# Loading v by heads, moving one step's second products, and shifting the w2 splits and a visit in a fused attention and mixture kernel

## The chip, the cores and the metric

The kernel runs on one core of a Trainium2 chip. The metric is the device time of one execution in microseconds (us). The kernel before was run three times: 449.62, 449.82 and 450.59 us, median 449.82 us.

## The reference

Four batches of four heads, 1088 positions and head dimension 32 go through a polynomial sketch attention; its output, 4352 tokens of 128 features, goes into a mixture of four two-layer experts with 1024 hidden units each.

```
phi(x)  = outer(S1 x, S2 x), flattened to 64 features      # S1, S2 are 8 x 32
kv      = sum over s of phi(k)_s v_s^T ;  z = sum over s of phi(k)_s
attn    = (phi(q) kv) / (phi(q) z + 1e-6)                  # per batch and head
x       = attn, heads side by side                         # 4352 x 128
p       = domain_probs / (sum of domain_probs + 1e-9)
out     = sum over e of p[:, e] * relu(x w1[e]) w2[e]      # 4 experts
```

Everything is fp32.

## The kernel before, in words

**The mixture.** The tokens are cut into chunks of 128, 448, 512, seven times 448, and 128. Each chunk takes sixteen steps: expert e is the step's number divided by four, and each step handles two blocks of 128 hidden units, one in each of two half-steps. Step i has half-steps 2i and 2i + 1, so half-step 33 is the second one of step 16, the first step of the second chunk. `first` makes the hidden units of a step. In the middle chunks w1 and x are split in three parts of shorter mantissa, and each block is three matmuls on TensorE (PE): L1175 and L1176 (names xa, wa and xb, wb), then, after ScalarE (ACT) has scaled the sum at L1177, L1227 (xd, wd). ScalarE then applies relu (L1231 or L1236), and VectorE (DVE) makes the lower parts of the hidden units (L1203 and L1206). In the first and the last chunk, called plain, the matmuls are plain fp32 and cut into halves of 64 rows or columns (`both` and `on_side`, L262).

**The second products.** `second` multiplies hidden units by w2 and adds up in a PSUM accumulator. The list `due` gives the half-step at which the second products of a step are issued. For plain chunks this is 2i + 5, but 2i + 7 for step 14 (`i == NQ - 2`), so that step 14's second products stand right before those of step 15 at half-step 35, eight instructions of 64 x 128 in all. With `w2` split in parts (`vab`, `vb`, `vd`), the later chunks use L1296 for the second products; in chunk 1 experts 0 and 1 use whole fp32 w2 (L1277). The parts of w2 are made by one split on ScalarE (L928, `vab<-w_sb`) and joins on DVE (L931: `vab`, `vb`, then `vd`), at the half-steps of `W2_AT`, one pair for each of the experts 2, 3, 0 and 1.

**The attention.** What is needed to start, the keys and values of batch 0 and its first queries, is made in `start`. Keys are turned (`kn` to `kT`), projected (fs) and multiplied (kp); `value_copy` spreads the values `vn` into `vx` on ScalarE (L423, L428), and PE sums kp times vx (L262, `h<-vx,kp`). The query factors are copied from PSUM (L1040, qb) and multiplied on DVE. Later work of the attention is cut into pieces with costs in a plan, which `work` hands out in half-steps. The units of queries after the first ones are the list `later`; the first of them (index w = 0; batch 0, 512 tokens) is called the third unit here. Its way is: its queries are turned and projected (`unit_project`, which writes `qs` to DRAM as `qd<-qs`, L790, and reads it back spread out, as `qp<-qd`, L797, and `qb<-qd`, L802), its two products are made on DVE (`unit_product`, L811), and its visit does the products `kvx` times `qp` on PE (L262) together with the projection `qT` times `sx` of the unit after it. `LAND` is 6: the third unit's products and visit are not handed out before LAND + 1 half-steps have passed since `unit_project`.

**The loads.** SyncE (SP) issues nearly all DMAs in program order: s_raw, k, q and v of batch 0, then the weights w1 (L159) and w2 (L172), then the k, q and v of later batches (`load_batch`: batch 1 after step 5, batch 2 after step 24), gates, and the `qd` traffic. `load_v` fills the tile `vn`, 128 partitions of 1088 floats. Partition 32a + g holds, for each head, positions 34g + 8a to 34g + 8a + 7; two small transfers (L137) bring the remaining two positions of each g. DMAs take eight semaphore lanes in turn, so the issue of one waits until the one that used its lane before, eight DMAs earlier, has landed.

Of the kernel before, what the change touches and what calls it, by code (L numbers as in the profile page):

```python
# [17 lines left out]
def _ap(t, p0: int, np_: int, off: int, free):  # L18

    p = list(t.ap)[0]  # L20
    return bass.AP(t.tensor, t.offset + p0 * p[0] + off, [[p[0], np_]] + [list(d) for d in free])
# [3 lines left out]
def kernel(  # L25
# [24 lines left out]
    nc = tc.nc  # L50
# [3 lines left out]
    B, H, S, D = q.shape  # L54
    E, DM, F = w1.shape
    R = 8
    R2 = 2 * R
    G = S // 32
# [3 lines left out]
    NQ = E * FB // 2  # L62
# [4 lines left out]
    LAND, EARLY = 6, 14  # L67
# [21 lines left out]
        ("b", 1, 1, 16), ("d", 1, 1, 17), ("b", 2, 0, 16), ("d", 2, 0, 17), ("b", 2, 1, 17), ("d", 2, 1, 18),  # L89
        ("a", 3, 1, 17), ("b", 3, 0, 19), ("b", 3, 1, 19), ("d", 3, 0, 20), ("d", 3, 1, 20),  # L90
    ]
    W2_AT = (36, 38), (41, 43), (45, 47), (65, 67)
    TOKENS_AT = 11, 12

    CHUNKS = [P, 448, 512] + [448] * 7 + [P]
# [32 lines left out]
    def load_v(b):  # L128
        t = lpool.tile([P, H * NT * D], F32, tag="vn", name="vn")
        base = v.offset + b * H * S * D  # L130
        for a in range(4):
            nc.sync.dma_start(
                _ap(t, 32 * a, 32, 0, [[8 * D, H], [1, 8 * D]]),
                bass.AP(v.tensor, base + 8 * a * D, [[G * D, 32], [S * D, H], [1, 8 * D]]),
            )
        for a in range(2):
            nc.sync.dma_start(  # L137
                _ap(t, 32 * a, 32, 1024, [[D, H], [1, D]]),
                bass.AP(v.tensor, base + (32 + a) * D, [[G * D, 32], [S * D, H], [1, D]]),
            )  # L140
        return t
# [35 lines left out]
    def in_three(b):  # L177
        return b in THREE
# [10 lines left out]
    def split_at(b):  # L189
        return (THREE if in_three(b) else OTHER).index(b)  # L190

    def second_weight(e, b):

        at = split_at(b)
        return w2_of[e, 0 if in_three(b) else 1][:, DM * at : DM * (at + 1)]
# [359 lines left out]
    def key_sums(b):  # L555
        sums[b] = held(psum(ps_h, "h"))
        for p in range(2):
            key_sum(b, p, sums[b])
# [207 lines left out]
    def unit_turn(w):  # L766

        b, c, n, u = later[w]
        turned[w] = query_turn(b, c, n)
        if w and u == len(UNITS[b]) - 1 and b + 1 < B:  # L770
            load_rows(q, b + 1, "qn")
# [36 lines left out]
    def unit_product(w, p):  # L808

        n, (qp, qb) = later[w][2], factors[w]  # L810
        nc.vector.tensor_tensor(out=qp[p][:, 0:n], in0=qp[p][:, 0:n], in1=qb[p][:, 0:n], op=ALU.mult)  # L811
# [12 lines left out]
    def vector_us(n):  # L824

        return 0.16 + n * 1.04e-3
# [3 lines left out]
    def add(cost, run, name, after=None):  # L830

        plan.append((cost, run, name, after))

    def lay_plan():

        of_first = queries(0, P, UNITS[0][1])
        costs = [0.62] * 9 + [0.05] * 4 + [0.4, 0.55, 0.6, 0.1, 0.1]
        distances = {12: ("first8", 3), 13: ("first12", 1), 16: ("first15", 2), 17: ("first16", 2)}
        for at, cost in enumerate(costs):
            add(cost, lambda: next(of_first, None), f"first{at}", distances.get(at))  # L840
        covers.append((len(plan), P + UNITS[0][1]))
        add(vector_us(later[0][2]), lambda: unit_turn(0), "qturn", ("start", 2 * NQ - 2))
        add(0, lambda: None, "wait", ("start", 2 * NQ + 2))
        keys = {}
        for b in range(1, B):
            now_on, plan[:] = list(plan), []
            key_pieces(b)
            keys[b], plan[:] = list(plan), now_on
        for w, (b, c, n, u) in enumerate(later):
            if b == 0:  # L850
                plan.extend(keys[1][:9])
            else:
                at = {(1, 0): (1, 9, 13), (1, 1): (2, 0, 3), (1, 2): (2, 3, 5), (2, 1): (3, 0, 3), (2, 2): (3, 3, 9)}
                if (b, u) in at:
                    k, z0, z1 = at[b, u]
                    plan.extend(keys[k][z0:z1])
                if b == 1 and u == 0:
                    blocked = key_end(b)
            more = w + 1 < len(later)
            if more:  # L860
                add(vector_us(later[w + 1][2]), lambda w=w: unit_turn(w + 1), "qturn")
            for p in range(2):
                add(vector_us(n), lambda w=w, p=p: unit_product(w, p), "product", ("visit", LAND if w else LAND + 1))

            last = 0 < b < B - 1 and u == len(UNITS[b]) - 1
            if last:
                plan.extend(keys[b + 1][(5, 9)[b - 1] :])

            def visit(w=w, more=more, then=b + 1 if last else None):
                if then:  # L870
                    key_sums(then)
                if w == 1:
                    key_sums(1)
                    blocked()
                if more:
                    unit_project(w + 1)
                unit_visit(w)

            add(0.1, visit, "visit", ("products" if last else "product", 3))
            if last:  # L880
                key_end(b + 1)
            add(0.4, lambda w=w: inverse.__setitem__(w, attend_inverse(*products[w])), "inverse", ("visit", 1))
            add(vector_us(n), lambda w=w: over.__setitem__(w, attend_scale(*products[w], inverse.pop(w))), "scale")
            add(vector_us(n), lambda w=w: unit_out(w), "out")
            covers.append((len(plan), S * b + c + n))
# [214 lines left out]
    hid, acc, total = {}, {}, {}  # L1100
    NP = FB // 2

    def plain(m):
        return m in (0, NC - 1)
# [133 lines left out]
    def second(i, j=None):  # L1238

        m, kq = steps[i]  # L1240
        n, (e, f) = CHUNKS[m], divmod(kq, NP)
        hd = hid[i]
        if plain(m):

            if f == 0:
                acc[m] = psum(ps_o, f"o{e % 2}")
            for j in range(2):
                for _ in range(2):
                    on_side(
                        lambda s: acc[m][half[s], 0:DM],  # L1250
                        lambda s: hd[j][:, HP * s : HP * s + HP],
                        lambda s: second_weight(e, 2 * f + j),
                        start=(f == j == 0),
                        stop=(f == NP - 1 and j == 1),
                    )
            if f == NP - 1:
                p_e = ends[:, 1 if m else 0, e : e + 1]
                if e == 0:
                    total[m] = mpool.tile([P, P], F32, tag="end", bufs=1, name="end")
                    nc.vector.tensor_scalar(  # L1260
                        out=total[m][:, :], in0=acc[m][:, 0:DM], scalar1=p_e, scalar2=None, op0=ALU.mult
                    )
                else:
                    nc.vector.scalar_tensor_tensor(
                        out=total[m][:, :], in0=acc[m][:, 0:DM], scalar=p_e, in1=total[m][:, :], op0=ALU.mult, op1=ALU.add
                    )
                if e == E - 1:
                    t, to = (B * S - P, [[DM, P], [1, DM]]) if m else (0, [[G * DM, 32], [1, 4 * DM]])
                    nc.sync.dma_start(bass.AP(out.tensor, out.offset + t * DM, to), total.pop(m)[:, :])
            return  # L1270
        if whole(m, e):
            if f == 0 and j == 0:
                acc[m, e] = None, psum(ps_o, f"o{e % 2}")
            for j in range(2) if j is None else (j,):
                k = 2 * f + j
                o1 = acc[m, e][1][:, 0:n]
                nc.tensor.matmul(o1, second_weight(e, k), hd[j], start=(k == 0), stop=(k == FB - 1))  # L1277
            return
# [119 lines left out]
    for what, e, h, step in SPLITS:  # L1398
        at_step(step, lambda p=(what, e, h): weight_part(*p))
    for e, at in zip((2, 3, 0, 1), W2_AT):  # L1400
        parts_of = second_weight_parts(e)
# [25 lines left out]
    due, closed = [], [None]  # L1427
# [19 lines left out]
    def to_due(i):  # L1447

        m, kq = steps[i]
        e, f = divmod(kq, NP)  # L1450
        if plain(m):
            due.append((2 * i + (7 if i == NQ - 2 else 5), 2 * i, 0, i, None, None))
        elif whole(m, e):
            late = (0, 0, 0, 0, 1, 1, 1, 1)[2 * f : 2 * f + 2] if e else (0, 0)
            due.extend((2 * i + 3 + j + late[j], 2 * i, j, i, j, None) for j in range(2))
        elif f == 0:
            for at, (p, slot) in enumerate(deal_of(m, e).items()):
                k = int(p[1])
                due.append((2 * i + slot, 2 * i, at, i + k // 2, k % 2, p[0]))
        due.sort(key=lambda d: d[:3])  # L1460

    for i in range(len(steps) + LA):
        if i < len(steps):
            m, kq = steps[i]
# [89 lines left out]
```

## Time and profile before

| | |
|---|---|
| median of three runs | 449.82 us (449.62 to 450.59) |
| the profiled execution | 449.77 us, span 448.0 us, so 1.77 us outside the span |
| granted TensorE clock | 1.0 in every slice |
| busy in the span | PE 99%, weight loads 83%, DVE 83%, ACT 75%, POOL 29% |
| first matmul of the mixture on PE | at 13.57 us |
| the v loads of batch 0 | issued 2.10 to 5.17 us, landed 6.15, 6.45, 6.78 and 7.91 us |
| the third unit's qd written | 37.5 and 38.08 us |
| its qb landed | 47.22 us (first set), about 50.5 us (second set) |

A row of the profile names the line of the kernel, the engine, the operation and `out<-in` with the names of the tiles. Times are from the start of the span. A bracket behind a row of the timeline is the time for which the engine stood idle before it and what released it. [...]

### The profile page before, as it was taken

How to read it: one execution, taken by the hardware profiler on the slowest of the kernel's cores; microseconds unless marked ns; L12 is line 12 of the kernel's file. 1: busy time of each engine (PE TensorE's matmuls, PEld its weight loads, DVE VectorE, ACT ScalarE, POOL GpSimd, SP SyncE). 2: the span in 40 equal slices, each digit the busy share in tenths (PEclk: the TensorE clock that was granted, in tenths of full speed). 3: DMA queues.
4: the chain of work that ended last, by engine and by line, in shares of the span. 5: the costliest groups of instructions: out<-in, count | busy, mean ns of one | idle time of the engine just before them, and what ended most of it. 6: DMA issues, size and time to landing. Idle time of an engine off the chain costs nothing.

```text
span 448.0 us, 8698 instructions
## 1 busy us (share of the span) xinstructions
PE 442.2 (99%) x3018; PEld 371.1 (83%) x3018; DVE 371.7 (83%) x634; ACT 334.0 (75%) x710; POOL 130.2 (29%) x211
## 2 busy tenths in 40 slices
PE   9999999999999999999999999999999999999997
PEld 6887678777778888888888888888888888888887
DVE  5998779986988896989879969898889898898853
ACT  4477778966867886778687868788788888888841
POOL 7346123310333132212321322123323313331440
PEclk9999999999999999999999999999999999999999
DMA  6965145014313502252252132421230021016501
GB/s 184 277 181 160 65 122 161 30 46 114 94 53 89 125 23 75 49 136 65 64 125 34 20 110 79 107 66 21 67 80 20 22 66 42 21 35 205 171 1 29
DMA packets 53619, 38.45 MB, mean 86 GB/s; under 512 B 26920, under 2 KB 49640, under 8 KB 53576
## 3 DMA queue, kind: packets, MB, share of 16 engines
q1 hardware_dynamic: 52776, 37.31, 31.4%
q0 software_dynamic: 576, 0.53, 0.5%
q8 instruction: 23, 0.38, 0.4%
q14 instruction: 20, 0.16, 0.1%
q10 hardware_dynamic: 224, 0.07, 0.1%
HBM read 32.68 MB, written 5.21 MB: 85 GB/s over the span
## 4 chain that ended last, share of the span: by engine, by line
PE 88%; DMA 4%; DVE 3%; SPq 2%; ACT 1%; issue 0%; POOL 0%; ACTq 0%; DVEq 0%; POOLq 0%
PE o L1296 40%; PE h L1227 13%; PE h L1175 13%; PE h L1176 13%; PE h L262 6%; PE o L262 2%; DMA qb<-qd 1%; DMA w_sb<-in_moe_w_dram 1%; SPq L172 1%; PE o L1277 1%; PE h L457 1%; DMA dp<-in_moe_domain_probs_dram 1%; DVE wb L931 1%; DVE wd L931 0%; DMA qd<-qs 0%
## 5 line engine op out<-in xcount | busy, mean ns | idle before, releaser
L1177 ACT ACTIVATE h<-h 128x448 f32<-128x448 f32 (+1 forms) x288 | 155.4, 540 | 72.0 <-PE h L1176 68.0
L1203 DVE SCALAR_TENSOR_TENSOR hb<-h,ha 128x448 fp32r<-128x448 f32 (+1 forms) x213 | 130.2, 622 | 39.2 <-ACT ha L1231 36.6
L1206 DVE SCALAR_TENSOR_TENSOR hd<-ha,hb 128x896 fp32r<-128x896 f32 (+2 forms) x111 | 123.5, 1113 | 11.3 <-PE o L1296 2.2
L1175 PE MATMUL h<-xa,wa 128*128 128x448 f32 (+1 forms) x288 | 131.4, 456 | 0.0
L1231 ACT ACTIVATE ha<-h 128x448 fp32r<-128x448 f32 (+1 forms) x213 | 116.6, 547 | 0.0
L1335 POOL TENSOR_TENSOR ev<-ev,gate 128x256 f32<-128x256 f32 (+1 forms) x54 | 47.6, 881 | 214.3 <-DVE ev L1328 205.4
L1227 PE MATMUL h<-xd,wd 128*128 128x448 f32 (+1 forms) x288 | 107.5, 373 | 1.1 <-ACT h L1177 1.0
L1176 PE MATMUL h<-xb,wb 128*128 128x448 f32 (+1 forms) x288 | 105.9, 368 | 0.0
L1296 PE MATMUL o<-ha,vab 128*128 128x448 f32 (+1 forms) x204 | 76.2, 374 | 0.0
L1175 PEld LDWEIGHTS h<-xa,wa 128*128 128x128 f32 x288 | 54.2, 188 | 18.2 <-issue 13.1
L1176 PEld LDWEIGHTS h<-xb,wb 128*128 128x128 f32 x288 | 54.2, 188 | 17.8 <-issue 13.7
L1227 PEld LDWEIGHTS h<-xd,wd 128*128 128x128 f32 x288 | 54.0, 188 | 10.9 <-ACT h L1177 4.2
L1296 PE MATMUL o<-hd,vd 128*128 128x448 f32 (+1 forms) x204 | 60.1, 369 | 0.0
L1296 PE MATMUL o<-hid,w_sb 128*128 128x448 f32 (+1 forms) x118 | 54.7, 545 | 0.0
L1296 PE MATMUL o<-hb,vb 128*128 128x448 f32 (+1 forms) x136 | 50.1, 368 | 0.0
L1337 POOL TENSOR_TENSOR total<-total,ev 128x256 f32<-128x256 f32 (+1 forms) x54 | 46.1, 854 | 4.2
L1236 ACT ACTIVATE hid<-h 128x448 f32<-128x448 f32 (+1 forms) x75 | 41.4, 552 | 1.0 <-PE h L1227 0.8
L1296 PEld LDWEIGHTS o<-ha,vab 128*128 128x128 f32 x204 | 38.3, 188 | 4.1
L1296 PEld LDWEIGHTS o<-hd,vd 128*128 128x128 f32 x204 | 38.1, 188 | 3.7
L1335 POOL TENSOR_TENSOR total<-ev,gate 128x256 f32<-128x256 f32 (+1 forms) x18 | 12.8, 730 | 70.7 <-issue 50.6
L1296 PEld LDWEIGHTS o<-hb,vb 128*128 128x128 f32 x136 | 25.5, 188 | 2.1
L1296 PE MATMUL o<-hb,vab 128*128 128x448 f32 (+1 forms) x68 | 25.3, 372 | 0.0
(153 smaller groups left out, 458.4 us busy)
## 6 DMA issues: line engine op xcount, KB each, us to landing
gate<-gates SPq DMA_DIRECT2D x22, 224.0 KB
kn<-in_k_dram SPq DMA_DIRECT2D x4, 544.0 KB
vn<-in_v_dram SPq DMA_DIRECT2D x16, 128.0 KB
w_last<-in_moe_w_dram SPq DMA_DIRECT2D x4, 512.0 KB
w_sb<-in_moe_w_dram SPq DMA_DIRECT2D x3, 512.0 KB
w_sb<-in_moe_w_dram SPq DMA_DIRECT2D x6, 256.0 KB
qp<-qd SPq DMA_DIRECT2D x6, 224.0 KB
qb<-qd SPq DMA_DIRECT2D x6, 224.0 KB
```

The lines of the kernel that those rows point to most:

```text
L262: nc.tensor.matmul(out(s), weights(s), moving(s), **flags)
L1175: nc.tensor.matmul(g, wa[:, e, w], xa, start=True, stop=False)
L1176: nc.tensor.matmul(g, wb[:, e, w], xb, start=False, stop=True)
L1177: nc.scalar.activation(g, g, ACTF.Copy, scale=1.0 + R12)
L1203: nc.vector.scalar_tensor_tensor(out=hb, in0=g, scalar=0.0, in1=high, op0=ALU.max, op1=ALU.subtract)
L1206: nc.vector.scalar_tensor_tensor(out=d2, in0=a2.bitcast(F32), scalar=R12, in1=b2.bitcast(F32), op0=ALU.mult, op1=ALU.subtract)
L1227: nc.tensor.matmul(g, w, x, start=False, stop=True, skip_group_check=True)
L1231: nc.scalar.activation(ha, g, ACTF.Relu, scale=NEAR)
L1236: nc.scalar.activation(hid[i][j], g, ACTF.Relu)
L1296: nc.tensor.matmul(acc[m, e][o][:, 0:n], w, h, start=first_one, stop=last)
L1335: nc.gpsimd.tensor_tensor(out=to[:, x], in0=ev[:, x], in1=g[:, x], op=ALU.mult)
L1337: nc.gpsimd.tensor_tensor(out=total[m][:, x], in0=total[m][:, x], in1=ev[:, x], op=ALU.add)
```

## The change

Three things change. `load_v` brings the values of a batch by heads: each of the four large transfers has one head, all 128 partitions, 256 floats for each. The source is read in four groups (a) of 32 rows (g). The runs stay 1 KB and the tile's contents stay the same. The second products of step 14 are due at 2i + 5 like the others of a plain chunk, and they are two matmuls on full 128 x 128 tiles in place of four on halves. `W2_AT` gives the splits of experts 3 and 0 one half-step less, and the third unit's products and visit wait LAND + 2 half-steps in place of LAND + 1.

```diff
-    W2_AT = (36, 38), (41, 43), (45, 47), (65, 67)
+    W2_AT = (36, 38), (40, 42), (44, 46), (65, 67)
...
     def load_v(b):
         t = lpool.tile([P, H * NT * D], F32, tag="vn", name="vn")
         base = v.offset + b * H * S * D
-        for a in range(4):
+        for h in range(H):
             nc.sync.dma_start(
-                _ap(t, 32 * a, 32, 0, [[8 * D, H], [1, 8 * D]]),
-                bass.AP(v.tensor, base + 8 * a * D, [[G * D, 32], [S * D, H], [1, 8 * D]]),
+                t[:, 8 * D * h : 8 * D * (h + 1)],
+                bass.AP(v.tensor, base + S * D * h, [[8 * D, 4], [G * D, 32], [1, 8 * D]]),
             )
...
             for p in range(2):
-                add(vector_us(n), lambda w=w, p=p: unit_product(w, p), "product", ("visit", LAND if w else LAND + 1))
+                add(vector_us(n), lambda w=w, p=p: unit_product(w, p), "product", ("visit", LAND if w else LAND + 2))
...
             for j in range(2):
+                if i == NQ - 2:
+                    o, w = acc[m][:, 0:DM], second_weight(e, 2 * f + j)
+                    nc.tensor.matmul(o, hd[j], w, start=False, stop=False)
+                    continue
                 for _ in range(2):
                     on_side(
...
         if plain(m):
-            due.append((2 * i + (7 if i == NQ - 2 else 5), 2 * i, 0, i, None, None))
+            due.append((2 * i + 5, 2 * i, 0, i, None, None))
```

On each engine the order moves as follows. On PE, two 128 x 128 instructions stand between L1176 and L1227 of half-step 33, the group of eight halves two half-steps later has four, and the third unit's visit stands one half-step later. On DVE, the joins `vab` and `vb` of an expert now stand ahead of the third unit's first product, where they stood behind it, and its second product stands ahead of the next expert's joins. On ACT, each L928 split of the two moved experts stands one half-step earlier.

## The prediction

> **What bounds the kernel now.** I read the busy times first, then what TensorE waited for, then the timelines around those waits, then DMA landings. The page's busy list and the waits of PE:
>
> ```profile
> PE 442.2 (99%) x3018; PEld 371.1 (83%) x3018; DVE 371.7 (83%) x634; ACT 334.0 (75%) x710; POOL 130.2 (29%) x211
> ```
>
> ```profile
> PE h L1227 <- ACT h L1177: 1.0, 2, 0.8
> ...
> PE h L262 <- DMA w_sb<-in_moe_w_dram: 0.5, 1, 0.5
> ```
>
> TensorE fills the span, the granted clock is full in every slice, and after about 58 us PE waits on nothing. So a microsecond comes or goes only by PE instructions saved or by a stall in the first 58 us. There the start is a chain of other engines and loads: first MoE matmul of PE at 13.57 us, and behind it the weights. The two L1227 waits are these (timeline of PE; start, duration, engine, line, operation, in brackets the idle time and its releaser):
>
> ```profile
> 29.80 0.36 PE L1176 MATMUL h<-xb,wb 128*128 128x448 f32 x1
> 30.37 0.47 PE L1227 MATMUL h<-xd,wd 128*128 128x448 f32 x1 [0.21 <-ACT h L1177]
> ...
> 49.27 0.37 PE L1176 MATMUL h<-xb,wb 128*128 128x448 f32 x1
> 50.39 0.47 PE L1227 MATMUL h<-xd,wd 128*128 128x448 f32 x1 [0.76 <-ACT h L1177]
> ```
>
> Undisturbed, L1227 starts 0.20 us after L1176 (30.88 to 31.08). So the first place loses 0.57 - 0.20 = 0.37 us, the second 1.12 - 0.20 = 0.92 us. The second has its cause in VectorE and ScalarE:
>
> ```profile
> 47.34 0.69 DVE L811 TENSOR_TENSOR qp<-qp,qb 128x512 f32<-128x512 f32 x1 [2.76 <-DMA qb<-qd]
> 47.95 0.42 DVE L931 SCALAR_TENSOR_TENSOR vab<-w_sb,vab 128x256 fp32r<-128x256 f32 x1
> 48.28 0.68 DVE L931 SCALAR_TENSOR_TENSOR vb<-w_sb,vab 128x512 fp32r<-128x512 f32 x1
> ```
>
> ```profile
> 49.06 0.85 ACT L928 ACTIVATE vab<-w_sb 128x768 fp32r<-128x768 f32 x1 [1.13 <-DVE vb L931]
> ```
>
> VectorE stood 2.76 us before a product whose factor had not landed, the w2 joins were queued behind it, ScalarE's split waited for them, and L1177, which PE needs, was queued behind the split.
>
> **Second products of step 14.** Eight half-width instructions of step 15's and 14's group become four there, and two full 128x128 ones stand before the L1227 that waited. Price: the sixteen half-width records of that group (one row of the PE timeline, 31.78, 1.09 us, 0.27 for one) run 0.055 us apart, two per instruction, so four instructions are 0.44 us; the full-width fp32 form has L457 as nearest row, 8 records of 0.89 us on the chain, four instructions, so two are 0.44 us. No saving in rate: the two lie in the 0.57 us gap, make the L1227 wait no more (0.20 + 0.44 = 0.64, 0.07 later than now), and 0.44 leaves the later group. Net -0.37 us (-0.27 to -0.5; a restart after a wait showed up to 0.1 us).
>
> **W2 splits and the visit.** The splits go one half-step earlier, the third unit's visit one later. On DVE the joins now stand ahead of the waiting product, so the split of 49.06 no longer waits: -0.92 us, and with it a smaller one at 57.36 (L1177 behind the split of 56.38, 0.15 us), together -1.07, with a restart -1.17. What hides the moved product: the second qp product starts at 50.63 when its factor lands, ends near 51.3; PE would come to the second kvx matmuls, a half-step later, near 51.3 to 51.8 once the stall is gone. That cover is thin: each microsecond by which the factors land later is a microsecond of PE wait. The later pieces move by a half-step; by the order on PE and ACT the small late stalls (0.17 at 80.31, 0.14 at 140.83) only move: 0, within 0.2 either way. The second joins are queued behind the second product, same term.
>
> **The v loads.** Four transfers of 128 KB remain, of 1 KB runs. Before: 32 partitions each, outermost loop of 32 on both sides. After: 128 partitions, but the source's outermost loop counts 4. The trace has such a form: the qb loads (L802, outermost source loop of 4). Windows of 1 us while they run (last two columns: share of the 16 DMA engines, GB/s), and the chain's piece:
>
> ```profile
> 46.00:47.00 1.00, 1.00 (x6) 0.77 (x5) 0.00 (x0) 0.94 (x4) 0.00 (x0) 1.00 0.26 100
> 47.00:48.00 1.00, 1.00 (x5) 0.61 (x4) 0.66 (x2) 0.93 (x2) 0.00 (x0) 1.00 0.26 98
> 48.00:49.00 1.00, 1.00 (x6) 0.66 (x4) 1.00 (x4) 0.00 (x0) 0.00 (x0) 1.00 0.26 98
> ```
>
> ```profile
> 40.88 6.34 DMA qb<-qd
> ```
>
> A share of 0.26 is four engines of 16, and each qb transfer ends with four engine completions on its semaphore, while an old v transfer ends with 16 and a gate load (outermost loop of 8) with 8. I take the count of the outermost loop as the number of engines: v would run on four. [...]
>
> Price: 512 packets over four engines, 128 each. A qb packet of 2 KB takes about 84 ns at 98 GB/s over four; by bytes 42 ns for 1 KB. The page's hardware queue gives 31.4% of 448.0 us x 16 for 52776 packets, 43 ns for a mean of 707 B; the line through that and 84 ns puts 1 KB at 52 ns. Old v packets, 16 engines at once, took 62 to 77. I take 47, between the nearest two: 6.0 us; the ends are 5.4 and 9.9. The engines are through with k and q at about 4.7 us (first completions of both: 4.3 to 4.9), so v lands at 10.7 (10.1 to 14.6) instead of 7.91. Need: the vx copies start at
>
> ```profile
> 8.35 0.63 ACT L423 COPY vx<-vn 128x512 f32<-128x512 f32 x1
> ```
>
> with 0.43 us of slack before PE's key sums feel it. Then fs, qb (L1040), kp, qp and all PE work shift by 10.7 - 8.35 - 0.43 = 1.9 us (1.3 to 5.8). Behind v on those four engines stand the last pieces of v and q and the first weights: their data began near 9.4, after near 11.6, +2.2 us. SP's queue counts as well: the first v transfer no longer waits for a landed k (now 1.7 us), but w1's and w2's issues (L159, L172) now wait for lanes that v holds; ScalarE's dp issues wait for s_raw, q and v lanes, hidden as they end before fs. PE waited 0.75 us (start to start) for w1 at 19.78, landing 20.45; with both delays near 2 that wait stays, so the larger one sets the shift: +2.2 us (0.9 to 5.8).
>
> Batch 1's v (issued 22.6 to 26.1 now) goes over four engines too, landing near 39 instead of 32.2. The gates, and the qd<-qs write of the third unit (issue 35.43, with the shift about 37.5, on a lane a v transfer holds), stand behind: 1.4 to 2 us later, so also qp, qb and the product. With the thin cover above PE then waits 0.5 to 1.0 at its kvx matmuls: +0.7 (0 to 3). Batches 2 and 3 load with several microseconds to spare: 0.
>
> Sum: +2.2 - 0.37 - 1.17 + 0.7 = +1.36. The profiled execution was 449.77 (span 448.0, 1.77 outside), 0.05 below the median 449.82: 451.13 for it, 451.2 for the median. My case's own range: 450.0 to 452.6.
>
> **The rivals.** *v still spreads over 16 engines* (faster): then it lands in time, the weights go out earlier, the w1 wait at 19.78 goes, capped at 0.35 since the kvx matmuls behind it wait for DVE's product at 20.50. -0.37 - 1.17 - 0.35 = -1.9: 447.9. For: 128 destination partitions, and only the source loop is short. Against: qb also had 32 partitions on its destination and got four. It decides if v lands before 8.8. [...]
>
> *Four engines, but quick, and no late qd* (same): at 42 ns v lands at 10.1, shift 1.3 to 1.5, -1.54 from the rest: 449.5 to 449.9. It needs the gates and qd to slip past v.
>
> *Four engines at the old packet time* (slower by more): landing at 12.6 to 14.6, shift 3.8 to 5.8, qd later by another 2: 453 to 456. For: the early v shares the memory with k and q. Against: with four engines fewer packets are in flight at once.
>
> *The joins' move does nothing* (part of the change fails): product and split only exchange places and PE waits 0.9 at kvx; my case plus 1.0, 452.2.
>
> **Chances.** My case 0.46 (with the fourth), 16 engines 0.20, quick 0.18, old packet time 0.16. What a measurement can tell from no change is 0.2%, 0.9 us. Of my case 0.04 falls under +0.9 and of the quick 0.05 above; faster 0.20, same 0.17, slower 0.63. The range takes the fast case's 447.9 and leaves out the upper part of the last: 447.9 to 454.0. Cases of both signs hold much; the likeliest one's own range is above.
>
> **What would show it.** DMA share near 0.25 from 5 to 10.7 us; L423 starting at 10 or later with a wait on vn; PE idle before L262 h<-vx,kp; PE's first x_first matmul near 15.5; no L1227 wait at the two places; L790 issued late, with kvx waiting for qp. If the share at 5 to 8 us stays above 0.6 and L423 stays at 8.4, v is not on four engines and my sum is wrong by 2.9 us. If L1227 waits again near 52, the joins' step is wrong.

## The result, and the profile after

The changed kernel takes 452.45 us (median of six runs, 451.46 to 453.35), the kernel before beside it 449.72 us (six runs, 448.62 to 450.59). The ratio is 1.0063, interval 1.0041 to 1.0084: 2.8 us slower, between 1.8 and 3.8. The profiled execution took 452.79 us, span 451.0.

The page's busy times and the waits of PE:

```profile
PE 443.1 (98%) x3014; PEld 372.3 (83%) x3014; DVE 371.4 (82%) x634; ACT 334.1 (74%) x710; POOL 125.9 (28%) x211
```

```profile
PE h L262 <- ACT vx L423: 3.4, 1, 3.4
...
PE h L262 <- DVE kvx L513: 0.3, 1, 0.3
PE h L262 <- DVE qp L610: 0.2, 1, 0.2
```

The two waits of L1227 and the one for w1 are gone; one wait of 3.44 us for the copies of v has come. The chain of work that ended last now runs through the last of the four v transfers, at its start:

```profile
3.97 7.99 DMA vn<-in_v_dram
12.74 3.87 PE h L262 x72
```

ScalarE's and PE's timelines say what hangs on it (in brackets the idle time before and its releaser):

```profile
12.06 0.63 ACT L423 COPY vx<-vn 128x512 f32<-128x512 f32 x1 [2.49 <-DMA vn<-in_v_dram]
```

```profile
12.74 0.49 PE L262 MATMUL h<-vx,kp 128*64 128x66 f32 x4 [3.44 <-ACT vx L423]
```

The copy was at 8.35 us and did not wait. Each v transfer's lane shows one semaphore event soon after its issue (3.20 us for the first, issued at 2.09) and four later ones, here called its completions; the last of the four, its landing, comes at 7.13, 8.54, 10.59 and 11.96 us. The windows (columns: the stretch and its length, then busy time of PE, PEld, DVE, ACT, POOL with counts, granted TensorE clock, share of the DMA engines, GB/s) show a share of 0.22 and 0.28, about four engines of 16, in two stretches in which little but v is in flight, an idle PE, and something that the prediction did not have, a clock cut to half:

```profile
5.00:6.00 1.00, 0.98 (x13) 0.38 (x13) 0.94 (x3) 0.70 (x2) 0.90 (x4) 1.00 0.22 53
...
10.00:11.00 1.00, 0.00 (x0) 0.00 (x0) 0.41 (x2) 0.00 (x0) 0.64 (x2) 1.00 0.28 91
11.00:12.00 1.00, 0.00 (x0) 0.00 (x0) 0.00 (x0) 0.00 (x0) 0.00 (x0) 1.00 0.91 147
12.00:13.00 1.00, 0.26 (x4) 0.26 (x6) 0.18 (x2) 0.94 (x3) 0.13 (x1) 0.77 0.61 238
13.00:14.00 1.00, 1.00 (x22) 1.00 (x22) 1.00 (x5) 0.67 (x3) 1.00 (x3) 0.50 0.79 292
14.00:15.00 1.00, 1.00 (x24) 1.00 (x23) 0.93 (x5) 0.00 (x0) 0.78 (x5) 0.50 0.76 221
15.00:16.00 1.00, 1.00 (x24) 1.00 (x24) 0.41 (x1) 0.00 (x0) 0.81 (x4) 0.52 1.15 291
```

A clock of 0.77, 0.50, 0.50 and 0.52 in these four windows makes 0.46, 1, 1 and 0.96 us at half clock, about 3.4 us.

The places of the old L1227 waits, in PE's timeline:

```profile
33.93 0.37 PE L1176 MATMUL h<-xb,wb 128*128 128x448 f32 x1
34.13 0.60 PE L1250 MATMUL o<-w_sb,hid 128*128 128x128 f32 x4
34.51 0.47 PE L1227 MATMUL h<-xd,wd 128*128 128x448 f32 x1
...
52.99 0.36 PE L1176 MATMUL h<-xb,wb 128*128 128x448 f32 x1
53.19 0.36 PE L1227 MATMUL h<-xd,wd 128*128 128x448 f32 x1
```

From L1176 to L1227 it is 0.58 us at the first place, with the two full-tile matmuls inside (0.57 before, without them), and 0.20 at the second (1.12 before). Where the same matmul stands in both profiled executions, the changed kernel's PE is late by 3.33 us at the first vx,kp (12.74 and 9.41), 4.88 at the first x_first (18.45 and 13.57), 4.15 at L1175 of half-step 32 (33.22 and 29.07), 3.71 four half-steps later, 2.43 once the visit is past (60.85 and 58.43 at L1175), 3.0 at the end.

### The profile page after: what moved, and what is told of

Same layout as the page of the kernel before. It is cut to its first block, busy times and chain, and to the rows that moved or that the text cites. A ratio compares the mean times of both kernels' runs of the same rounds, so it can differ in the third digit from the quotient of the medians.

```text
span 451.0 us, 8694 instructions
## 1 busy us (share of the span) xinstructions
PE 443.1 (98%) x3014; PEld 372.3 (83%) x3014; DVE 371.4 (82%) x634; ACT 334.1 (74%) x710; POOL 125.9 (28%) x211
## 4 chain that ended last, share of the span: by engine, by line
PE 94%; DVE 2%; DMA 2%; SPq 1%; issue 0%; ACT 0%; ACTq 0%; DVEq 0%
PE o L1300 40%; PE h L1227 13%; PE h L1175 13%; PE h L1176 13%; PE h L262 7%; PE o L1281 3%; PE o L262 2%; DMA vn<-in_v_dram 2%; PE h L457 1%; DVE qp L610 0%; SPq L132 0%; DVE qa L903 0%; PE h L1145 0%; DVE hd L1206 0%; DVE rd L642 0%
## 5 line engine op out<-in xcount | busy, mean ns | idle before, releaser
L1177 ACT ACTIVATE h<-h 128x448 f32<-128x448 f32 (+1 forms) x288 | 155.3, 540 | 71.7 <-PE h L1176 67.3
L1206 DVE SCALAR_TENSOR_TENSOR hd<-ha,hb 128x896 fp32r<-128x896 f32 (+2 forms) x111 | 123.4, 1112 | 10.4 <-PE o L1300 1.6
L1175 PE MATMUL h<-xa,wa 128*128 128x448 f32 (+1 forms) x288 | 131.4, 456 | 0.0
L1227 PE MATMUL h<-xd,wd 128*128 128x448 f32 (+1 forms) x288 | 107.2, 372 | 0.1
L1339 POOL TENSOR_TENSOR ev<-ev,gate 128x256 f32<-128x256 f32 (+1 forms) x54 | 46.1, 854 | 216.5 <-DVE ev L1332 206.7
L1176 PE MATMUL h<-xb,wb 128*128 128x448 f32 (+1 forms) x288 | 105.9, 368 | 0.0
L1175 PEld LDWEIGHTS h<-xa,wa 128*128 128x128 f32 x288 | 54.2, 188 | 18.3 <-issue 12.9
L1176 PEld LDWEIGHTS h<-xb,wb 128*128 128x128 f32 x288 | 54.2, 188 | 17.7 <-issue 13.7
L1227 PEld LDWEIGHTS h<-xd,wd 128*128 128x128 f32 x288 | 54.0, 188 | 8.5 <-ACT h L1177 2.0
L1341 POOL TENSOR_TENSOR total<-total,ev 128x256 f32<-128x256 f32 (+1 forms) x54 | 43.9, 813 | 4.2
```

What stands on the lines that cost most here:

```text
L1175: nc.tensor.matmul(g, wa[:, e, w], xa, start=True, stop=False)
L1176: nc.tensor.matmul(g, wb[:, e, w], xb, start=False, stop=True)
L1177: nc.scalar.activation(g, g, ACTF.Copy, scale=1.0 + R12)
L1206: nc.vector.scalar_tensor_tensor(out=d2, in0=a2.bitcast(F32), scalar=R12, in1=b2.bitcast(F32), op0=ALU.mult, op1=ALU.subtract)
L1227: nc.tensor.matmul(g, w, x, start=False, stop=True, skip_group_check=True)
L1339: nc.gpsimd.tensor_tensor(out=to[:, x], in0=ev[:, x], in1=g[:, x], op=ALU.mult)
```

## The experiments

The theory: the source's outermost loop of four puts each v transfer on four DMA engines, and that alone makes the kernel slower; the rest gains. The rivals: loading by heads or onto 128 partitions is slow in itself, and a second one, that the two other parts gain only in a kernel whose start is late. Ratios are against the kernel before, run beside the others; in 25, 22 and 11 such runs its median was 449.16, 449.32 and 449.41 us. A difference in us is the ratio's distance from 1 times that median. The ratios are not the quotients of the two medians and lie up to 0.0007 from them.

**The changed kernel with the old v loads (e1_old_v).**

```diff
-        for h in range(H):
+        for a in range(4):
             nc.sync.dma_start(
-                t[:, 8 * D * h : 8 * D * (h + 1)],
-                bass.AP(v.tensor, base + S * D * h, [[8 * D, 4], [G * D, 32], [1, 8 * D]]),
+                _ap(t, 32 * a, 32, 0, [[8 * D, H], [1, 8 * D]]),
+                bass.AP(v.tensor, base + 8 * a * D, [[G * D, 32], [S * D, H], [1, 8 * D]]),
```

> The changed kernel with the old v loads. Theory (the v loads on four engines cost all that is lost, the other two parts gain what the trace of after shows, 0.43 and 1.28 us): the start is that of before, first mixture matmul near 13.6 us, no L1227 wait at half-steps 33 and 44, and the time is 449.7 - 1.7 = 448.0 us (447.7 to 448.4). Rival (the two parts gain only because the late start gave DVE and DMA time to run ahead): the stall near 50 us comes back in another place and the time is 449 to 449.7 us.

448.06 us, ratio 0.9969 (0.9957 to 0.9981): 1.4 us faster than before (0.9 to 1.9; 1.1 by the medians). That is the theory's time and not the 449 to 449.7 us of the rival: the two other parts gain with an early start too. Sixteen completions for each v transfer where the change had four, L423 at 8.3 us, no L1227 wait. This version beats both kernels.

**Only the v loads (e2_v_only).** The diff of e1 the other way, on the kernel before.

> The kernel before with only the new v loads. Theory: v lands near 12 us, PE idles over 3 us and then runs at half clock, the first mixture matmul comes near 18.4, the wait for w1 near 19.8 is gone (-0.7): 449.7 + 4.1 = 453.9 us, up to 454.4 with the late drift seen in after. Rival (as in the prediction: a delay that the weights and later waits swallow): 451.5 to 452.5 us.

452.87 us, ratio 1.0076 (1.0061 to 1.0090): 3.4 us slower (2.7 to 4.0; 3.7 by the medians). That lies between the two expectations: the v loads cost here somewhat less than the theory's 4.1. In its profiled run v landed at 10.9, PE waited 2.04 us and the clock stayed at 1.0; two of its six runs had a mean clock of 0.996, and they are the slowest (453.49 and 453.70). The wait of L1227 for the split stayed, and grew:

```profile
52.79 0.47 PE L1227 MATMUL h<-xd,wd 128*128 128x448 f32 x1 [1.27 <-ACT h L1177]
```

**Only the second products (e3_second_only).**

```diff
+                if i == NQ - 2:
+                    o, w = acc[m][:, 0:DM], second_weight(e, 2 * f + j)
+                    nc.tensor.matmul(o, hd[j], w, start=False, stop=False)
+                    continue
...
-            due.append((2 * i + (7 if i == NQ - 2 else 5), 2 * i, 0, i, None, None))
+            due.append((2 * i + 5, 2 * i, 0, i, None, None))
```

> The kernel before with only the second products of step 14 in full tiles at half-step 33. Theory (they fill the wait before L1227): 0.4 us less, 449.3 us (449.1 to 449.5). Rival (the wait for L1177 only moves or the gain is taken by the stall near 50 us, whose end is set by a DMA): no change, 449.7.

449.28 us, ratio 1.0001 (0.9990 to 1.0012): no gain. The time itself is the theory's, but the kernel before took 449.16 us beside it, so the ratio speaks for the rival. The trace says why. Against before, PE is 0.44 us early at half-step 32 (run to run, below), 0.87 early at half-step 36, so the part does its 0.43; and 0.41 early after this row:

```profile
49.98 0.47 PE L1227 MATMUL h<-xd,wd 128*128 128x448 f32 x1 [1.22 <-ACT h L1177]
```

The wait that was 0.76 us is 1.22. Behind it stand the split, the joins, the product and at the end a qb load. It landed at 46.80 us where it was 47.22, so 0.42 us earlier, while PE came 0.87 earlier. The rival was right: alone, the gain is given back 15 us later.

**Only the w2 splits and the visit (e4_shift_only), and each of the two (e7_w2_only, e8_visit_only).**

```diff
-    W2_AT = (36, 38), (41, 43), (45, 47), (65, 67)
+    W2_AT = (36, 38), (40, 42), (44, 46), (65, 67)       # e4, e7
...
-    ... ("visit", LAND if w else LAND + 1))
+    ... ("visit", LAND if w else LAND + 2))              # e4, e8
```

> The kernel before with only the w2 splits and the third unit's visit shifted. Theory (joins ahead of the waiting product): the wait of 0.92 us at 49.3 and the one of 0.15 at 57.4 go, 1.1 to 1.3 us less, 448.5 us. Rival (thin cover: the second product's factor lands at 50.5 and PE comes to kvx too early): a wait for qp of 0.3 to 0.8 us at the kvx matmuls, 449.0 to 449.4 us.

> The kernel before with only the w2 splits shifted, the visit as before. Theory (it is the order of the joins before the product that removes the stall): the first product now waits behind or ahead of joins by its own due time; joins first: the stall of 0.92 goes, but PE comes to the visit earlier and waits for qp's second half, landing 50.5: net gain 0.3 to 0.9 us. Rival (the visit's shift does it all): no change, 449.7.

> The kernel before with only the third unit's products and visit one half-step later. Theory: the products come behind the joins of experts 3 but ahead of those of expert 0 in half; the stall of 0.92 us goes or halves, 0.4 to 1.1 us less. Rival (the splits' shift does it all): no change, 449.7.

Both: 448.42 us, ratio 0.9979 (0.9970 to 0.9987), 0.9 us faster (0.6 to 1.3), somewhat less than the theory's 1.1 to 1.3. The visit alone: 448.84, ratio 0.9990 (0.9981 to 0.9999), 0.45 faster, at the low end of its theory. The splits alone: 449.94, ratio 1.0011 (1.0002 to 1.0020), 0.5 slower, which neither the theory nor the rival had. All three traces have lost the 0.92 us wait at the split. In the one with the splits alone PE is 1.63 us ahead of before at that L1227, 0.7 of it from the start; then two long waits in PE's timeline take that away, and it is 0.2 behind:

```profile
50.88 0.69 PE L262 MATMUL h<-kvx,qp 128*64 128x66 f32 x16 [0.37 <-DVE qp L811]
...
70.31 0.47 PE L1227 MATMUL h<-xd,wd 128*128 128x448 f32 x1 [1.14 <-ACT h L1177]
```

```profile
69.20 0.63 ACT L928 ACTIVATE xa<-ring 128x512 fp32r<-128x512 f32 x1 [1.23 <-DMA ring<-xd]
```

The first is the thin cover of the prediction: the visit, not shifted, comes before the second product. At the second, an L1177 is queued behind ScalarE's split of the next chunk's x, which waits for its load (ring<-xd). That load landed at 69.18 us, 68.66 in the kernel before, while PE was 1.14 ahead; why it did not come earlier with PE was not followed. In the two kernels with the visit shifted neither shows. So the shift of the visit is the part that pays. That the splits add to it beside it is likely and not shown: the intervals of e4 and e8 overlap.

**A loop of 32 written as 4 times 8 (e6_loop48).**

Against the kernel of e1:

```diff
-                bass.AP(v.tensor, base + 8 * a * D, [[G * D, 32], [S * D, H], [1, 8 * D]]),
+                bass.AP(v.tensor, base + 8 * a * D, [[8 * G * D, 4], [G * D, 8], [S * D, H], [1, 8 * D]]),
```

> The changed kernel with the old v loads (32 partitions each, all heads, same bytes and packets), but the source's outer loop of 32 written as 4 times 8. Theory (the count of the outermost loop is the number of engines): each transfer ends with four engine completions, v lands near 11 to 14 us, time within 1 us of the changed kernel (452.5). Rival (it is the order by heads or the 128-partition destination that makes the new loads slow): v lands near 8 us with 16 completions and the time is that of the changed kernel with old v loads, near 448.

448.03 us, ratio 0.9970 (0.9958 to 0.9982), the four v transfers landed by 8 us, with 16 completions for each transfer. By the numbers that is the rival's outcome, but the run does not tell the two apart: with 16 completions and not the change's four, the run says nothing of transfers on four engines. The outer step is eight inner steps, so the two loops are one even loop of 32, and the 16 completions are those of that loop in e1. It is e1 again.

**Heads and 128 partitions, with other outermost loops (e9_heads8, e10_heads16).** Same transfers, packets and destinations as in the change; only the source positions differ. Both read other positions of v than the attention needs, so they serve for their times alone.

```diff
-                bass.AP(v.tensor, base + S * D * h, [[8 * D, 4], [G * D, 32], [1, 8 * D]]),
+                bass.AP(v.tensor, base + S * D * h, [[4 * G * D, 8], [8 * D + 16, 16], [1, 8 * D]]),   # e9
+                bass.AP(v.tensor, base + S * D * h, [[8 * D + 16, P], [1, 8 * D]]),                    # e10
```

> The changed kernel, v by heads on 128 partitions as there (same four transfers, same 1 KB packets, same destinations), but the source read in an outermost loop of 8 instead of 4, which takes other positions, so keys meet wrong values. Theory (the outermost count sets the engines): eight completions for each transfer, some 0.75 us each instead of 1.5, the last landing near 8.4 to 9.2, vx copies start 8.4 to 9.3, no clock drop, time 448.0 to 449.0. Rival (order by heads or 128 partitions makes the loads slow): v lands near 12 as in the changed kernel, 452.5.

> As the one with an outermost loop of 8, but with one loop of 128 over overlapping positions (wrong values again), same transfers, packets and destinations. Theory: 16 completions for each transfer, the last v landing at 7 to 8 us, the start of the kernel before, time 448.0 (447.6 to 448.5). Rival: v lands near 12, time 452.5.

e10: 447.94 us, ratio 0.9969 (0.9958 to 0.9980). The four transfers landed at 5.59, 5.99, 6.33 and 6.70 us, with 16 completions each, and ScalarE's copy was back in its place, without a wait:

```profile
8.07 0.63 ACT L423 COPY vx<-vn 128x512 f32<-128x512 f32 x1
```

Loading by heads onto all partitions is no slower than the old loads; against the changed kernel on the same chip (451.87, below) only the source's loops and the addresses that they walk through differ, and the difference is 3.9 us. The addresses are nearly consecutive in e10 and 4352 bytes apart in the change. But in the old loads too each partition's runs start 4352 bytes behind the last one's, and those ran with 16 completions and landed by 7.91 us, so runs that lie apart are not slow in themselves. What is left is the loop of four, with its four completions. e9 was meant to run on eight engines. It showed 16 completions and 447.70 us, ratio 0.9963 (0.9949 to 0.9976): 16 times 272 floats are 4352, just its outer step, so it too is one even loop, of 128. So no v load ended with eight completions, and what eight engines would cost was not measured.

**Matmuls in the gap (e5_fill, e12_fill), and the changed kernel again (e11_after).**

```diff
-        for i in range(3):
+        for i in (0, 1, 2) * 3:
             for j in range(2):
                 both(fq[i][:, 0:n], sr[:, i, j, :], qT[:, 0:n], start=(j == 0), stop=(j == 1))
```

> The changed kernel with the start's query projection done three times over (same result), so that TensorE has some 3 us of matmuls in the gap in which it waits for v. Theory (the granted clock fell because PE stood idle): clock 1.0 from 9 to 17 us, the 72 vx,kp matmuls take 2.3 us instead of 3.8, the first mixture matmul comes 1.5 us earlier, of which the wait for w1 takes back up to 0.7: 0.8 to 1.5 us less than the changed kernel. Rival (the low clock has another cause): clock 0.5 in 13 to 16 us as before, the same time as the changed kernel.

> The changed kernel itself, beside the others on one chip. Theory: v lands near 11 to 12 us with four completions a transfer, time 452.5 (451.8 to 453.3); runs whose mean granted clock is 1.0 about 0.7 us below those with 0.996.

> The changed kernel with the query projection done three times, again, on the same chip as the changed kernel. Theory (the idle stretch of TensorE lowers its clock): 0.8 to 1.5 us less than the changed kernel, clock 1.0 in all runs. Rival (the lower clock costs little, since PE waits for w1 a little later anyway): within 0.3 us of it.

e5: 451.35 us, ratio 1.0042 (1.0029 to 1.0054). On one chip, e11: 451.87 us, ratio 1.0053 (1.0040 to 1.0065); e12: 451.26 us, ratio 1.0039 (1.0025 to 1.0052). The mean clock was 0.999 or 1.0 in all ten filled runs, and 0.996 in nine of the eleven runs of the changed kernel. On the one chip the filled kernel is 0.6 us faster. That lies between the theory's 0.8 to 1.5 and the rival's 0.3, and the intervals overlap, so the fill shows that the clock stayed up with matmuls in the gap, and not well what the clock costs. In e12's profiled run, the slowest of its five, PE still waited 0.70 us for v, and the wait for w1 came back in its old place:

```profile
24.14 0.66 PE L262 MATMUL h<-x_first,w_sb 128*64 128x128 f32 x8 [0.49 <-DMA w_sb<-in_moe_w_dram]
```

A second look at the price is within the changed kernel: its two runs with the mean clock at 1.0 are the fastest of their sets, 451.46 against 452.14 to 453.35 and 450.95 against 451.78 to 452.19 us. The changed kernel's profiled run e11, at 450.95 us the fastest of its five, kept the full clock after a shorter wait, and the 72 matmuls took 2.32 us instead of 3.82:

```profile
11.99 2.32 PE L262 MATMUL h<-vx,kp 128*64 128x66 f32 x72 [2.81 <-ACT vx L423]
```

## Why the prediction was right

The forecast of slower by 1.4 us held in sign and mechanism. The measured 452.45 us lies 1.25 above its 451.2, near the upper end of its likeliest case (450.0 to 452.6). That it lies so near is in part luck: the start term was 1.7 too small, and the term of batch 1's v, 0.7, did not come. Its steps:

- **The engine count** was right: four completions and a share of 0.22 to 0.28 in the quiet windows. Taking the count of the outermost loop for the number of engines was the author's estimate from qb; the runs show four completions for the source's loop of 4 in the change, sixteen for the loop of 32 in e1 and the one of 128 in e10. e6 and e9, sixteen each, fit only if their two loops count as the one even loop that they make. What the early single event on each lane of the change stands for no run shows. The transfer with eight completions that the prediction calls a gate load is the write `gates<-pt` (L367); the loads `gate<-gates` end with sixteen.
- **The price of the load** was right in its rate: e11's transfers end 1.43, 1.59 and 1.57 us apart, 48 ns for each packet if 32 of them go over each of four engines, where 47 was taken; the rival with the old packet time (62 to 77) is out. The landing was 0.5 to 1.3 us later than 10.7, as the first transfer's data ended only at 6.6 to 7.1. The start term (+2.2) is the one that was mis-sized: 3.9 us by e11 against e10, and still 3.3 by e12 against e10, where the clock was held.
- **What the term lacked** was the clock. With PE's wait of 3.44 us the granted clock went to 0.5 for about 3.4 us, and the delay grew from 3.33 us at the first vx,kp to 4.88 at the first x_first. With the waits of 2.81 us (e11) and 2.04 us (e2) the clock stayed at 1.0; what decides between them no run here shows. It is part of the excess and not all: with the clock held by the fill, the kernel is still 1.8 to 1.9 us slower than before.
- **The w1 wait** of 0.75 us at 19.78 did not stay: it is in neither trace of the changed kernel, where PE came still later than the weights. It was also no fixture of the kernel before: e3, e4 and e8, with the same start, do not have it and reach half-step 32 at 28.2 to 28.6 us and not at 29.07. The profiled execution used for the sum had a late start, and the 2.2 was counted from it.
- **Second products** (-0.37): 0.43 in the trace, but 0.0 alone (e3). The forecast counted the parts as if each gain stood by itself; this one stands only where the stall near 49 us is gone.
- **Splits and visit** (-1.17): 1.28 in the traces of before and after, 0.9 timed alone, and with the second products 1.4 (e1) where 1.54 was summed. The thin cover was where it was said to be: e7 shows the wait for qp that the shifted visit avoids. What the prediction put at nothing is the pieces that move by a half-step behind it. In the change, e1, e4, e8 and every other kernel with the shifted visit, DVE now does a hidden-unit instruction of 1.23 us (L1206) right before `kvx` (L513, at 104.43 us in the change), where it stood behind it, and PE waits there. From the projection to the visit it is 1.18 us in place of 0.75, so 0.43 is lost; in e2, e3 and e7, whose visit is not shifted, it is 0.75 or 0.76 (PE before, PE after, DVE after):

```profile
100.05 0.93 PE L262 MATMUL h<-qT,sx 128*64 128x224 f32 x8
100.80 1.10 PE L262 MATMUL h<-kvx,qp 128*64 128x66 f32 x32
```

```profile
103.60 0.93 PE L262 MATMUL h<-qT,sx 128*64 128x224 f32 x8
104.78 1.15 PE L262 MATMUL h<-kvx,qp 128*64 128x66 f32 x32 [0.25 <-DVE kvx L513]
```

```profile
103.29 1.23 DVE L1206 SCALAR_TENSOR_TENSOR hd<-ha,hb 128x1024 fp32r<-128x1024 f32 x1
```
- **Batch 1's v and the late qd** (+0.7): did not come. Its last v transfer landed at 35.55 us, not near 39, as the first of the four ended at 31.39 (31.08 before) and the others some 1.4 us apart. That was ahead of the qd writes at 39.98, which were late mostly because PE was. DVE stood 1.19 and 1.16 us before its two products, and kvx did not wait for them:

```profile
51.88 0.69 DVE L811 TENSOR_TENSOR qp<-qp,qb 128x512 f32<-128x512 f32 x1 [1.19 <-DMA qb<-qd]
...
55.20 0.78 DVE L811 TENSOR_TENSOR qp<-qp,qb 128x512 f32<-128x512 f32 x1 [1.16 <-DMA qb<-qd]
```

What stays open: the later part of the span gives back another 0.5 to 0.6 us in the traces of the change and e1 (2.43 us late after the visit, 3.0 at the end; e1 is 2.55 ahead of before there, 0.85 of it from the start, and 2.06 at the end). The 0.43 at kvx is most of it; the remaining 0.1 or so was not followed. What the lowered clock costs is known only roughly: some 0.6 us by the fill, 1.1 by the runs within the changed kernel, in which v may also have landed sooner.

## What to carry to other kernels

Before a DMA's access pattern is rewritten, look at the outermost loop of its source: here a loop of four, which did not make one even loop with the one inside it, left each v transfer with four completions in place of 16, and the load in front of the first matmuls cost 3.9 us, while writing to all 128 partitions was no loss (e10 and e1, ratio 0.9969 each). A gain in front of a stall whose end is set by a transfer, like the 0.43 us of the second products, was no gain until that stall was gone, so parts of a change are summed along the path and not one by one. And a long wait of PE can cost more than its length: with the one of 3.44 us came a clock of 0.5, with those of 2.04 (e2) and 2.81 (e11) it stayed at 1.0.

## What the runs showed of the hardware

The clock was not foreseen: in the change's profiled run 3.44 us of PE waiting, and a granted clock of 0.5 until about 16 us; with matmuls in the gap (e5, e12) its mean stayed at 0.999 or 1.0 in ten of ten runs. Two loops that step as one, the outer step being all the inner steps together, were as good as one loop: 4 times 8 (e6) and 8 times 16 (e9) both ended with 16 completions, at 448.03 and 447.70 us. And 128 partitions bought no time over 32: e10's first three transfers landed some 0.5 us sooner than the old ones (5.59, 5.99 and 6.33 against 6.15, 6.45 and 6.78 us), and its ratio is that of e1, 0.9969.
